# Attention weight gradients of a transformer backward pass: first loads moved into the last backward step, modulation gradients moved beside the last weight-gradient chunks

## Chip, cores, metric

One core of a Trainium2 chip. The metric is the device time of one execution in microseconds, lower is better; medians of several runs are given, and a profile of one execution of each kernel. The changed kernel and all experiments were measured against the kernel before on the same chip in alternating rounds. The rounds ran on several chips, so compare medians only within one round, and ratios across rounds.

## The reference

The program computes a forward pass and all its gradients: adaptive LayerNorm, an attention layer that walks over 64 segments of 32 tokens with 8 memory rows carried from segment to segment, and a gated feed-forward layer. Cut to what matters here:

```
q, k, v = h @ Wq, h @ Wk, h @ Wv         # 32 heads of 128, D = 512, rows h = 8 memory + 32 tokens
o = softmax(mask(q @ k.T)) @ v
out = o @ Wo ;  mem = out[:, :8]         # memory of the next segment
h = layernorm(x) * (1 + ca) + sa         # sa, ca, ... = silu(c) @ w_mod
# wanted here: dWo = o^T dy, dWq/dWk/dWv = h^T dq/dk/dv, dx through LayerNorm, dc, dw_mod
```

The backward pass over the segments is serial. When it has ended, the sums over all segments remain: the four weight gradients, the last LayerNorm's backward, and the gradients of `c` and `w_mod`. This last stage is what the change touches.

## The kernel before

PE = TensorE, DVE = VectorE, ACT = ScalarE, POOL = GpSimd, SP = SyncE. PSUM holds TensorE's sums in banks; an evacuation is the copy of a finished sum out of its bank by ACT or DVE. A load is issued by an engine's queue and has landed when all its data are there. "Half clock" is time in which TensorE was granted half of its clock. A backward step keeps the transposed weights in one pool:

```
self.WqT = wp.tile([128, H, D], BF16); self.WkT = ...; self.WvT = ...
self.WoT = wp.tile([128, DC, H * E], BF16)
```

The last stage (names: `dyrows` = gradient of the attention output by rows, `hrows` = attention input by rows, `rows` = per-head rows read from DRAM: OSR for o, DQR/DKR/DVR for dq/dk/dv):

```
hrows  = build_side_rows(self.H1ROWS, ...)      # 2.6 MB, half on SP's queue, half on ACT's
dyrows = build_side_rows(self.DAROWS, ...)      # 2.6 MB
load_rows(0); load_rows(1)                      # lp: three buffers of up to 2.6 MB
for i, (_, kind, outw, (hl, g0, ng)) in enumerate(todo):      # 9 o chunks, then 27 q/k/v chunks
    load_rows(i + 2)
    rows = loaded.pop(i)
    while ln_done[0] * len(todo) < i * NT and ln_done[0] < NT:
        ln_step()                               # one of 16 LayerNorm tiles
    if kind == "qkv":  ...                      # gps  <- hrows, rows  (4 x 20 matmuls of 128x512)
    else:                                       # gps5o <- dyrows, rows (20 matmuls a head)
        for gg in range(ng):
            ps = psG.tile([128, D], F32, tag="g")                        # 4 PSUM banks
            for tp_ in range(NTP):
                nc.tensor.matmul(ps[:], lhsT=rows[:, tp_, gg*E:(gg+1)*E], rhs=dyrows[:, tp_, :], ...)
            ot = op_.tile([128, D], BF16)                                # 3 output buffers
            self.evac(next_eng(), ot[:], ps[:])                          # ACT and DVE in turn
            nc.gpsimd.dma_start(outw[h0 + 3 * gg], ot[:])
...   # LayerNorm's last tiles, accs -> DMOD; pools close
...   # modulation gradients: dmod_bc, w_mod load; 4 x (dwm on DVE/ACT, junk on DVE); dc
```

One LayerNorm tile loads x0 (one DMA), dhb (eight small DMAs) and dx1 (one) on SP's queue, works on DVE, POOL and ACT, and adds two matmuls into a PSUM sum:

```
x0  <- x_rows;  bn_stats/bn_aggr/rstd/xh from x0
dhb <- DHA, DHB
nc.tensor.matmul(acc_ps, lhsT=sel[:, 0, :], rhs=dhb)
pr = dhb * xh                                   # POOL
nc.tensor.matmul(acc_ps, lhsT=sel[:, 1, :], rhs=pr)
dx1 <- DX1ROWS; dx0 = ln_bwd_rows(...); store
```

In these traces, what an engine is held by also holds what comes after it on the same engine (in e5 below, an evacuation stood 11.55 us behind load issues). The framework's scheduler decides that order from the source's order and from its own model of when data will be there.

## Time and profile before

| stage of the profiled run (us) | before |
|---|---|
| R, end of the last backward step (last dh_tps matmul) | 3051.2 |
| R to the first weight-gradient matmul | 47.8 |
| first to last weight-gradient matmul | 563.7 |
| of it, PE idle / at half clock | 1.0 / 4.7 |
| last matmul to the end of the span | 33.6 |
| R to the end of the span | 645.1 |

Median 3693.76 us of 3 runs (3689.59 to 3695.60). These dates are read from the instruction records of the trace. R itself moves by more than 10 us from one profile to the next, for reasons upstream (the seven steps before the last take 15 to 24 us each, not the same ones long each time). So all comparisons below use the time from R to the end, which no upstream scatter enters. Two profiles of the same changed kernel agree in it within 2 us; every other kernel has one profile, so a difference of 2 or 3 us between kernels says little.

### The profile page before, as it was taken

The numbers are of one execution on the slowest core, as the hardware profiler recorded it, in microseconds if no ns is written. First come the engines' busy times: TensorE is split into PE (matmuls) and PEld (weight loads), VectorE is DVE, ScalarE is ACT, GpSimd is POOL, SyncE is SP. The second block draws the span as 40 slices with busy tenths as digits, with TensorE's granted clock in tenths as the row PEclk, the third lists the DMA queues.
The fourth block names the chain that finished last, engine by engine and source line by source line (L and its number), as shares of the span: only waits on it lengthen the run. The fifth ranks groups of instructions, "written<-read, shape, count | busy, mean of one in ns | idle before, by whom it ended". The sixth has DMA issues, their size and how long they took to land.

```text
span 3696.3 us, 108208 instructions
## 1 busy us (share of the span) xinstructions
PE 3282.3 (89%) x45566; PEld 1897.6 (51%) x45566; DVE 1640.8 (44%) x4087; ACT 1208.9 (33%) x2742; POOL 957.9 (26%) x1917
## 2 busy tenths in 40 slices
PE   1889888899999969996989999999999994999996
PEld 1445444455555535553546666666666662445453
DVE  2454444455545556663225445444455541222222
ACT  0444444444544444442123333333333330000001
POOL 3333333333333323331111112111221221222221
PEclk6999999999999989998999999999999997999998
DMA  7565656566666653324779999999999998787774
GB/s 235 122 134 127 137 131 131 138 137 141 143 139 148 144 163 123 121 102 151 231 213 236 230 228 228 226 223 217 238 246 233 235 212 201 206 207 196 200 197 149
DMA packets 809259, 667.20 MB, mean 181 GB/s; under 512 B 511082, under 2 KB 683898, under 8 KB 808644
## 3 DMA queue, kind: packets, MB, share of 16 engines
q1 hardware_dynamic: 718948, 501.39, 60.5%
q0 software_dynamic: 31024, 103.06, 9.0%
q10 hardware_dynamic: 58800, 55.84, 5.8%
q8 instruction: 357, 5.85, 0.7%
q14 instruction: 130, 1.06, 0.1%
HBM read 292.82 MB, written 275.02 MB: 154 GB/s over the span
## 4 chain that ended last, share of the span: by engine, by line
PE 53%; DMA 5%; issue 3%; DVE 3%; ACT 1%; SPq 1%; POOL 0%; DVEq 0%; ACTq 0%; POOLq 0%
PE gps L1372 11%; PE dh_ps L208 10%; PE proj_ps L1138 6%; PE g_ps L1171 4%; PE gps5o L1382 3%; PE gps L941 3%; PE mm L855 3%; PE dh_tps L208 2%; PE tps L1103 2%; DMA Kst<-KST 2%; PE mm L788 1%; PE mm L792 1%; PE dp_ps L1161 1%; PE dp_ps L1157 1%; PE pass_ps L435 1%
## 5 line engine op out<-in xcount | busy, mean ns | idle before, releaser
L1372 PE MATMUL gps<-rows,hrows 128*128 128x512 bf16 (+2 forms) x2160 | 417.1, 355 | 0.0
L1372 PEld LDWEIGHTS <-hrows 128*128 128x128 bf16 x2160 | 211.4, 98 | 204.2
L647 POOL TENSOR_TENSOR Pst<-Pst,rden 120x1408 bf16<-120x1408 bf16 x64 | 162.7, 2542 | 415.4 <-DMA Pst<-ET 347.3
L1138 PE MATMUL proj_ps<-dyT,WoT 128*128 128x40 bf16 x8192 | 233.1, 180 | 19.4 <-issue 11.8
L1138 PEld LDWEIGHTS <-WoT 128*128 128x128 bf16 x8192 | 223.6, 96 | 30.6 <-issue 30.4
L63 DVE CAST ot<-gps 128x512 bf16<-128x512 f32 (+3 forms) x77 | 48.9, 635 | 395.2 <-PE gps L1372 259.7
L435 PEld LDWEIGHTS <-hT 128*32 128x32 bf16 x6144 | 140.5, 97 | 156.9 <-ACT hT L638 22.4
L234 DVE TENSOR_TENSOR dh_lo<-dh_ps,dh_hi 128x256 bf16<-128x256 f32 x128 | 48.4, 420 | 344.0 <-ACT dh_hi L230 344.0
L1382 PE MATMUL gps5o<-dyrows,rows 128*128 128x512 bf16 x640 | 141.4, 383 | 45.4 <-DMA rows<-OSR 45.4
L61 ACT ACTIVATE ot<-gps 128x512 bf16<-128x512 f32 (+3 forms) x77 | 42.4, 551 | 418.1 <-PE gps L1372 262.5
L208 PE MATMUL at_ps<-Wo,OT 128*32 128x512 bf16 x2048 | 135.0, 384 | 27.9 <-ACT OT L61 25.4
L61 ACT ACTIVATE dVT<-g_ps 128x512 bf16<-128x512 f32 (+1 forms) x192 | 107.8, 561 | 157.3 <-PE g_ps L1171 119.2
L208 PE MATMUL dh_ps<-WvT,dVT 128*32 128x512 bf16 x2048 | 151.8, 391 | 4.6 <-issue 4.5
L1376 POOL DMA_DIRECT2D out_dram<-ot x108 | 81.2, 752 | 281.9 <-DVE ot L63 153.5
L61 ACT ACTIVATE dOT<-proj_ps 128x480 bf16<-128x480 f32 (+2 forms) x192 | 68.4, 391 | 257.8 <-PE proj_ps L1138 250.5
L61 ACT ACTIVATE dQT<-g_ps 128x512 bf16<-128x512 f32 (+1 forms) x192 | 107.8, 561 | 125.1 <-PE g_ps L1171 125.1
L63 DVE CAST dKT<-g_ps 128x512 bf16<-128x512 f32 (+1 forms) x192 | 123.7, 644 | 44.0 <-PE g_ps L1171 43.2
L63 DVE CAST RAq<-pass_ps 128x512 bf16<-128x512 f32 x128 | 88.4, 691 | 121.8 <-PE pass_ps L435 121.8
L234 DVE TENSOR_TENSOR at_lo<-at_ps,at_hi 128x256 bf16<-128x256 f32 x128 | 48.4, 420 | 211.9 <-ACT at_hi L230 211.9
L61 ACT ACTIVATE OT<-tps 128x512 bf16<-128x512 bf16 (+1 forms) x192 | 101.0, 560 | 122.5 <-PE tps L559 91.1
L208 PE MATMUL dh_ps<-WkT,dKT 128*32 128x512 bf16 x2048 | 136.7, 388 | 0.0
L435 PE MATMUL pass_ps<-Wv,hT 128*32 128x512 bf16 x2048 | 126.8, 391 | 9.4 <-ACT hT L638 9.4
(364 smaller groups left out, 7230.7 us busy)
## 6 DMA issues: line engine op xcount, KB each, us to landing
OSR<-Ost SPq DMA_DIRECT2D x64, 352.0 KB
OT<-OT SPq DMA_DIRECT2D x64, 352.0 KB
PS<-Pst SPq DMA_DIRECT2D x64, 352.0 KB
OT_l<-OT SPq DMA_DIRECT2D x64, 352.0 KB
Pst_l<-PS SPq DMA_DIRECT2D x64, 352.0 KB
DVR<-rows_x POOLq DMA_DIRECT2D x64, 352.0 KB, 5.0
DKR<-rows_x POOLq DMA_DIRECT2D x64, 352.0 KB, 6.4
DQR<-rows_x POOLq DMA_DIRECT2D x64, 352.0 KB, 4.7
```

The lines of the kernel that those rows point to most:

```text
L61: return nc.scalar.activation(out, in_, AF.Copy)
L63: return nc.vector.tensor_copy(out, in_)
L208: self.nc.tensor.matmul(ps[32 * j:32 * j + 32, :], lhsT=lhsT, rhs=w, start=(n < 4), stop=(n >= total - 4), tile_position=(0, 32 * j))
L234: nc.vector.tensor_tensor(lo[:], ps[:, 256 * h:256 * h + 256], parts[h][:], op=ALU.subtract)
L435: nc.tensor.matmul(ps[32 * j:32 * j + 32, :], lhsT=lhs(c), rhs=rhs, start=(c == 0), stop=(c == DC - 1), tile_position=(0, 32 * j))
L647: nc.gpsimd.tensor_tensor(Pst[0:120, :, :], Pst[0:120, :, :], rden[:, :].unsqueeze(2).to_broadcast([120, G, 128]), op=ALU.mult)
L855: nc.tensor.matmul(hp[:], lhsT=xT[:, fc, :], rhs=wT[:, fc, :], start=(n == 0), stop=(n == 2 * FC - 1))
L941: nc.tensor.matmul(ps[:], lhsT=h2r[:, j, c * 128:(c + 1) * 128], rhs=xr[:, j, :], start=(j == 0), stop=(j == NT - 1))
L1138: nc.tensor.matmul(ps[:, g_, hl * L:(hl + 1) * L], lhsT=WoT[:, c, h * E:(h + 1) * E], rhs=dyT[:, c, :], start=(c == 0), stop=(c == DC - 1))
L1171: nc.tensor.matmul(ps[:, j, :], lhsT=lh[:, g * GW:(g + 1) * GW], rhs=rh[:, g * GW:(g + 1) * GW], start=True, stop=True)
L1372: nc.tensor.matmul(ps[:, 0:ng * E], lhsT=hrows[:, tp_, c * 128:(c + 1) * 128], rhs=rows[:, tp_, 0:ng * E], start=(tp_ == 0), stop=(tp_ == ...
L1382: nc.tensor.matmul(ps[:], lhsT=rows[:, tp_, gg * E:(gg + 1) * E], rhs=dyrows[:, tp_, :], start=(tp_ == 0), stop=(tp_ == NTP - 1))
```

## The change

Its intent: (1) put the transposed Wo first in the pool and the new row tiles over it, so that the first loads can start while the last backward step still runs; (2) load only what the first chunk needs (chunk 0 split into 2 + 2 heads) and bring hrows later, beside chunks 1 and 2; (3) run LayerNorm's 16 tiles over 31 chunks in place of 36 and do the modulation gradients, one step a chunk, beside the last six.

```diff
+        self.WoT = wp.tile([128, DC, H * E], BF16, name="WoT")
         self.WqT = wp.tile([128, H, D], BF16, name="WqT")
...
-        self.WoT = wp.tile([128, DC, H * E], BF16, name="WoT")
...
         with ExitStack() as ctx:
+            rp = ctx.enter_context(tc.tile_pool(name="p5g_r", bufs=1))
+            dyrows = rp.tile([128, NTP, D], BF16, name="dyrows")
+            rows_a = rp.tile([128, NTP, 2 * E], BF16, name="rows5a")
+            zrow = rp.tile([1, M // 2, D], BF16, name="zrow")
+            ...                                  # rows_a, then dyrows, on both queues, first of all
...
+            def mod_grads(step):                 # 0: accs -> DMOD, dmod_bc; 1..4: w_mod tiles; 5: dc
...
-                hrows = build_side_rows(self.H1ROWS, "hrows", mem_h)
-                dyrows = build_side_rows(self.DAROWS, "dyrows", mem_dy)
+                hrows = rp.tile([128, NTP, D], BF16, name="hrows")
+                o_chunks = [(0, 0, 2), (0, 2, 2)] + chunks[1:]
...
-                load_rows(0)
                 load_rows(1)
+                load_rows(2)
+                n_ln = len(todo) - 6
                 for i, ... in enumerate(todo):
                     load_rows(i + 2)
+                    if 1 <= i <= 2:
+                        load_h(i - 1)
                     rows = loaded.pop(i)
-                    while ln_done[0] * len(todo) < i * NT and ln_done[0] < NT:
+                    while ln_done[0] * n_ln < i * NT and ln_done[0] < NT:
                         ln_step()
+                    if i >= n_ln:
+                        mod_grads(i - n_ln)
...
-            ...                                  # the old modulation gradients behind the loop
```

## The prediction

> **What bounds the kernel now.** I read the page's 40 slices first. PE is at 8 or 9 tenths nearly everywhere; after the start the lowest digits are a 6 in slices 15 and 19 (not touched by this change), a 4 in slice 34 (3050 to 3142 us) and a 6 in the last. In these two something is waited for. I then read the chain that ended last in its last 650 us, which crosses both holes:
>
> ```profile
> 3045.83 5.37 PE dh_tps L208 x96
> 3051.64 12.98 DMA hrows<-H1ROWS
> 3064.64 2.77 DMA hrows<-AOA
> 3067.43 11.25 DMA dyrows<-DAROWS
> 3082.22 5.93 SPq L1357
> 3088.20 7.76 SPq L1357
> 3096.00 14.95 DMA x<-in_A_x_dram
> ...
> 3636.68 26.01 PE gps L1372 x160
> 3662.69 30.74 issue
> ```
>
> Columns: start, length (us), what. The last backward step ends at about 3051.2 (its tail matmuls, dh_tps). Then one load stands behind another (hrows, dyrows, rows) and PE does nothing until 3099.0. From there matmuls follow each other to 3662.7, and the last 31 us have none. Who waited, for the weight-gradient stage and then for the issue queue of SyncE at its start (total us, times, longest):
>
> ```profile
> PE gps5o L1382 <- DMA rows<-OSR: 45.4, 1, 45.4
> PE acc_ps L1288 <- POOL pr L1287: 1.0, 1, 1.0
> ...
> SPq L281 <- PE dh_tp L255: 8.0, 1, 8.0
> SPq L1336 <- DMA dyrows<-DAROWS: 8.0, 1, 8.0
> ```
>
> So the whole stage has one big wait, 45.4 us, and almost none later: 563.7 us from first to last matmul, about 2 of them lost. SyncE itself was held 8.0 us until 3051.24: its first load of this stage lies over the backward step's weights. The tail, from the timeline:
>
> ```profile
> 3662.81 0.35 SPq L1398 DMA_DIRECT2D dmod_bc<-DMOD  x1
> 3670.65 2.85 ACT L1407 ACTIVATE dwm<-dmod_bc,scT 128x3072 bf16<-128x3072 f32 x1 [7.56 <-DMA dmod_bc<-DMOD]
> 3677.79 3.36 DVE L1410 SCALAR_TENSOR_TENSOR junk<-wmod,dmod_bc 128x3072 bf16<-128x3072 bf16 x1 [5.32 <-DMA wmod<-in_w_mod_dram]
> 3689.36 3.35 DVE L1410 SCALAR_TENSOR_TENSOR junk<-wmod,dmod_bc 128x3072 bf16<-128x3072 bf16 x1
> 3693.97 0.28 SPq L1424 DMA_DIRECT2D out_dram<-dc_rows  x1
> ```
>
> The modulation gradients load only at 3662.8, though their input (accs stored to DMOD at 3637.4) was ready 25 us before: their pools open after the matmuls' pools close. Last matmul to end of span: 3696.3 - 3662.7 = 33.6 us.
>
> **What the Trainium skill says.** "DMA: Bandwidth & Descriptors", Queues, rings and completion order, says that SP and ACT each own a ring on the same 16 engines, served in turn; its Anatomy of one DMA says that a wait is done by the issuing sequencer before dispatch. So a load waiting in a queue holds all behind it, and two queues share bandwidth. The trace agrees: with one queue feeding, the windows show some 200 GB/s, with both 340:
>
> ```profile
> 3085.00:3087.00 2.00, 0.00 (x0) 0.00 (x0) 0.00 (x0) 0.00 (x0) 0.00 (x0) 0.50 1.15 203
> 3093.00:3095.00 2.00, 0.00 (x0) 0.00 (x0) 0.00 (x0) 0.00 (x0) 0.00 (x0) 0.50 1.10 346
> ```
>
> The same page's Specifications put line rate at transfers of 512 B or more. The trace differs a little: the 512 B pieces of a two-head chunk (3201 to 3205) moved at 255 GB/s, against 346 for 1 KB. The Anatomy's fixed 2 us also shows: an undisturbed 64 KB store took 2.1 us to land. "TensorE: Matmul & The Clock Gate", What's actually happening, gives about 3.4 us at half clock after idling; here the first 20 matmuls took 6.8 us (3099.0 to 3105.8) instead of 4.3. That is paid in both kernels.
>
> **The change, part by part.** (1) *Early loads over the freed dO weights.* The source puts WoT first in its pool and the new rows and dyrows tiles over it, so that they could load from 3032.5, where the last step finishes with WoT. The built program says otherwise: the first of these loads on SyncE waits for the last tail matmul against WqT, the very wait that held ca_bc until 3051.24, and ACT's half stands behind the last dh_b_hi evacuation (3051.5). I take the pools, not the tiles, to be what is waited for. So I give the early start nothing.
>
> (2) *What is loaded before the first matmul.* Before: hrows 2.62 MB, dyrows 2.62 MB and four heads of rows 2.62 MB, partly shared with the next chunk. After: two heads of rows (1.31 MB) and dyrows; hrows goes behind chunks 1 and 2. The clock: data flow from about 3053.3 (as H1ROWS did). Rows 1.31 MB at 255 GB/s: 5.1 us, to 3058.4. DAROWS 2.10 MB took 10.8 us from issue to landing both times before (H1ROWS: 3051.6 to 3062.4; DAROWS: 3067.4 to 3078); queued behind the rows without a gap it needs 7 us of flow, so it lands at about 3066. Then the small pieces: in the built program the loads of both queues take eight DMA semaphores in rotation, and each waits until its semaphore's last user has landed; so the second DHA piece on SyncE waits for ACT's DAROWS, ACT's zero row for SyncE's DAROWS. Before, that ending took 3 us of issues (3078 to 3081); now three DHA pieces and the zero row at 0.75 us each, to 3069, and 2.1 us to land: first matmul at 3071 instead of 3099.0. Gain 28.
>
> (3) *What is given back.* The first LayerNorm tile's matmul stands, in PE's order, after 154 of the stage's matmuls, i.e. 6.8 + 134 x 0.2165 = 35.8 us after the start, at 3106.8. Its dhb loads stand on SyncE behind hrows, and by the same rotation one waits for ACT's half of chunk 4, which ACT issues only after its second evacuation (about 3091.5) and behind its 1.05 MB half of H1ROWS. Estimate from the rates above: rows 1 to 3 (5.9 MB) to 3091, H1ROWS to 3097, ACT's half of chunk 4 (1.31 MB, one queue, 200 GB/s) to 3104 and landing 3105; two more waits of 2 to 2.5 us in the chain: dhb at 3110, pr 1 us later. PE waits about 5 us there, against 2 before. ACT, held by its hrows pieces until about 3108, still evacuates before PE needs the bank (four banks of 4.3 us). Later chunks have 17.3 us for 2.62 MB (151 GB/s), as before. Cost 3.
>
> (4) *Tail.* In the built program step 0 falls at chunk 30, the four w_mod steps around chunks 31 and 32 (two w_mod loads far earlier, among the dO-weight chunks), the final transpose before the last chunk. Per step ACT 2.85 us and DVE 3.4 us, while each evacuates one 0.6 to 0.7 us tile in 8.6: DVE was busy 2.9 of 26.7 us at the old end, so there is room. The added 1.57 MB broadcast and 6.3 MB of w_mod and out_11 fall in about 90 us in which DMA moved 160 GB/s: room too. What remains behind the last matmul is one evacuation (0.4), the issue (at +0.7) and the landing of a 64 KB store (2.1 to 2.5): 3.2 us instead of 33.6. Gain 30.4. (5) LayerNorm over 31 chunks instead of 40 and chunk 0 as 2+2 heads: the same matmuls, no cost.
>
> Sum: 28 - 3 + 30.4 = 55 us, 1.5%. 3693.8 - 55 = 3639.
>
> **Rivals.** (a) The loads do start at 3032.5: then rows and DAROWS land under the backward step, only DHA and the zero row remain after 3051.3, first matmul near 3059, time 3627. For it: source and title. Against: the built wait, which I trust; 5%. Even that stays within 2%. (b) The wait moves: LayerNorm's first tiles and the rows behind hrows starve PE by 10 to 15 us instead of 5, since 11 MB must pass in the first 45 us and two queues now wait for each other. For it: before, those tiles' loads stood behind nothing but rows; against: before, PE lost only 2 us with the DMA equally full. Time 3646 to 3651; 20%. (c) The modulation work stalls PE late: dmod_bc arrives late, ACT (which waits for it in order) holds its evacuations past four banks. For: DMOD's store queues behind 1.31 MB of rows. Against: I count 16 us from the accumulator's end to dmod_bc, with about 20 available before the evacuation behind it is due. 3 to 8 us; 15%. (d) Nothing gained in front because bandwidth is conserved: hrows' 2.62 MB must still move, but in about 140 us of dO-weight chunks which need 151 of 230 GB/s, so it hides. Against this rival; 5%.
>
> **Range and chances.** First matmul 3068 to 3076, given-back waits 0 to 12, end behind the last matmul 3 to 6, run scatter 3 each way: 3630 to 3650 should hold it 8 times in 10. 2% faster is 3619.9, a gain of 74; all idle time of both holes is 48 + 33.6 = 82, and the loads and the last store can't be free, so faster has 0.02. Slower would need a new 130 us: 0.01.
>
> **What would show it.** The first weight-gradient matmul at 3071, waiting for dyrows or its zero row, with SyncE's first load issued at 3051 and not at 3033 (else step 1 is wrong, rival a). One wait of PE of some 5 us for dhb about 36 us later (step 3). No PE wait above 2 us in the last 100 us, w_mod multiplies among the evacuations, and 3 to 4 us between last matmul and end (step 4). The prediction is wrong if PE's waits within the stage sum to over 15 us, or if a new wait stands at the first q chunk for hrows.

## The result, and the profile after

The changed kernel takes 3653.19 us (median of 4: 3650.16 to 3660.49) against 3694.68 (4 runs). The ratio is 0.9893, with a 95% interval of 0.9874 to 0.9911. Ratios here are the mean time of one kernel's runs over that of the other's of the same rounds, so not quite the ratio of the medians. In later rounds the same kernel took 3662.09 (6 runs) against 3691.24, ratio 0.9910 [0.9879, 0.9940]. It is 1% faster, where 1.5% was predicted, and the first median lies 3 us above the predicted range.

| us | before | after | after, repeated | predicted |
|---|---|---|---|---|
| R to first matmul | 47.8 | 23.5 | 19.9 | 19.8 |
| first to last matmul | 563.7 | 581.6 | 583.1 | 567 |
| PE idle in it | 1.0 | 13.9 | 15.5 | 5 |
| at half clock in it | 4.7 | 15.7 | 15.3 | as before |
| last matmul to end | 33.6 | 4.2 | 4.2 | 3.2 |
| R to end | 645.1 | 609.3 | 607.3 | 590 |

The gain from R to the end is 35.8 us (24.3 - 17.9 + 29.4) in the first profile and 37.8 in the second. The span of the first profile is 47 us shorter than before's; the 11 us beyond the 35.8 are R, which came earlier there. The two ratios, which take in all runs and the stages before R, come to 39 and 33 us, so there is no sign that the change gained or lost anything before R.

The chain that ended last, kernel after, its longest pieces before 3125, same columns as before:

```profile
3040.93 15.09 DMA dyrows<-DAROWS
3064.00 27.47 DMA rows<-OSR
3092.98 9.69 DMA x<-in_A_x_dram
3110.95 13.71 DMA rows<-OSR
```

The end of the backward step is followed by one 15 us load of dyrows, where before there were hrows, dyrows and rows in a row. But the chain does not then go over to matmuls, as it did before: it goes on, with short pieces between, through loads until after 3124. The waits, first of SyncE's queue around the stage's start, then of PE over the whole stage:

```profile
SPq L1263 <- PE dh_tp L255: 8.9, 1, 8.9
SPq L275 <- DMA hrows<-H1ROWS: 5.3, 1, 5.3
```

```profile
PE gps5o L1423 <- DMA dyrows<-zrow: 20.7, 1, 20.7
PE acc_ps L1304 <- POOL pr L1303: 5.8, 4, 2.6
PE acc_ps L1301 <- DMA hrows<-AOA: 4.7, 1, 4.7
PE acc_ps L1301 <- DMA dhb<-DHB: 1.8, 2, 1.2
```

The first load (line 1263) waited until the last step had ended, so nothing started early. Line 275 is the first piece of LayerNorm's dhb: SyncE could not issue it for 5.3 us, until an H1ROWS load had landed. The one big wait is 20.7 us instead of 45.4. New are the small ones, nearly all at LayerNorm's two matmuls (lines 1301 and 1304); by their dates all of 0.6 us or more lie in the first 130 us after R. The longest, in the timeline of DVE, ACT and PE:

```profile
3102.69 0.69 DVE L1290 BATCH_NORM_STATS2 st<-x 128x6 f32<-128x512 bf16 x1 [12.65 <-DMA x<-in_A_x_dram]
3105.24 0.60 ACT L61 ACTIVATE ot5o<-gps5o 128x512 bf16<-128x512 f32 x1 [19.96 <-DMA hrows<-AOA]
3105.64 0.58 PE L1301 MATMUL acc_ps<-dhb,sel 128*128 128x512 bf16 x1 [4.74 <-DMA hrows<-AOA]
3108.49 0.58 PE L1304 MATMUL acc_ps<-pr,sel 128*128 128x512 bf16 x1 [1.41 <-POOL pr L1303]
```

DVE stands 12.65 us for x0 and PE 4.74 us for dhb; ACT is idle for 20 us, the last 11.5 or so behind its own hrows issues (an estimate: the sum that it evacuates was complete at about 3093.7, 4.3 us after the one before). The releaser named for PE's wait is the transfer that arrived last by the profile; the matmul itself reads dhb. The eight pieces of dhb were issued from 3099.7 to 3103.8, behind the 5.3 us shown above and behind hrows, whose first issue alone held SyncE's queue for 9.32 us (0.53 us for the other half on ACT's queue). After it the matmuls run at half clock until 3113. The engines and the transfers in 10 us windows of the kernel after (busy times, then granted clock, DMA share, GB/s):

```profile
3070.00:3080.00 10.00, 9.13 (x43) 3.99 (x42) 0.69 (x1) 0.60 (x1) 1.08 (x2) 1.00 1.14 285
3080.00:3090.00 10.00, 9.87 (x46) 4.31 (x46) 1.35 (x2) 0.60 (x1) 1.08 (x2) 1.00 1.10 298
3090.00:3100.00 10.00, 9.95 (x47) 4.56 (x47) 0.03 (x1) 0.00 (x0) 0.54 (x1) 1.00 1.09 248
3100.00:3110.00 10.00, 3.63 (x11) 1.17 (x10) 5.64 (x13) 1.41 (x2) 2.86 (x4) 0.66 0.64 140
```

and of the kernel before, at about the same distance from its first matmul (3099.0):

```profile
3110.00:3120.00 10.00, 10.00 (x48) 4.57 (x47) 5.42 (x15) 1.68 (x3) 1.99 (x4) 1.00 0.27 87
3130.00:3140.00 10.00, 10.00 (x48) 4.51 (x46) 5.45 (x12) 1.29 (x2) 4.14 (x7) 1.00 0.49 129
```

After, the DMA share is 1.1 for 30 us on end while the o chunks run and PE then runs dry. Before, the windows at 0.27 and 0.49 stand between others at 1.05 to 1.10. Over the first 90 us after R the mean share is 0.82 before and 0.97 after, the rate 203 and 220 GB/s. (A share of 1.1 is no fixed rate: in the prediction's two windows it went with 203 and with 346 GB/s.) The tail, kernel after:

```profile
3645.22 0.38 ACT L61 ACTIVATE ot<-gps 128x256 bf16<-128x256 f32 x1 [3.98 <-PE gps L1413]
3645.89 0.72 POOL L1417 DMA_DIRECT2D out_dram<-ot  x1 [1.37 <-ACT ot L61]
```

One evacuation and one store end the program, as predicted.

### The profile page after: what moved, and what is told of

The parts are those of the page before. It is cut to its first block, busy times and chain, and to the rows that moved or that the text cites. A ratio compares the mean times of both kernels' runs of the same rounds, so it can differ in the third digit from the quotient of the medians.

```text
span 3649.4 us, 108148 instructions
## 1 busy us (share of the span) xinstructions
PE 3275.7 (90%) x45490; PEld 1897.2 (52%) x45566; DVE 1636.2 (45%) x4085; ACT 1214.5 (33%) x2744; POOL 963.1 (26%) x1917
## 4 chain that ended last, share of the span: by engine, by line
PE 42%; DMA 11%; issue 6%; DVE 4%; POOL 2%; ACT 2%; SPq 0%; ACTq 0%; POOLq 0%; DVEq 0%
PE dh_ps L208 10%; PE proj_ps L1138 6%; PE g_ps L1171 4%; PE gps L941 3%; PE mm L855 3%; PE dh_tps L208 2%; PE gps5o L1423 2%; PE tps L1103 2%; DMA rows<-DKR 2%; DMA Kst<-KST 2%; PE gps L1413 1%; PE mm L788 1%; DMA x<-in_A_x_dram 1%; PE mm L792 1%; PE dp_ps L1161 1%
## 5 line engine op out<-in xcount | busy, mean ns | idle before, releaser
L63 DVE CAST dKT<-g_ps 128x512 bf16<-128x512 f32 (+1 forms) x192 | 123.4, 643 | 37.8 <-PE g_ps L1171 37.4
L1423 PE MATMUL gps5o<-dyrows,rows 128*128 128x512 bf16 x588 | 133.0, 384 | 1.8 <-DMA rows<-OSR 0.8
L435 PE MATMUL pass_ps<-Wq,hT 128*32 128x512 bf16 x2048 | 134.0, 382 | 0.0
```

The lines of the kernel that those rows point to most:

```text
L63: return nc.vector.tensor_copy(out, in_)
L435: nc.tensor.matmul(ps[32 * j:32 * j + 32, :], lhsT=lhs(c), rhs=rhs, start=(c == 0), stop=(c == DC - 1), tile_position=(0, 32 * j))
L1423: nc.tensor.matmul(ps[:], lhsT=rows[:, tp_, gg * E:(gg + 1) * E], rhs=dyrows[:, tp_, :], start=(tp_ == 0), stop=(tp_ == NTP - 1))
```

## The experiments

18 kernels ran on the chip. Totals of one kernel scatter by some 10 us either way (the kernel before: 3678 to 3713 in all rounds). "Idle" is PE's idle time between first and last weight-gradient matmul, split into the first 90 us after R, the rest of the o chunks, and the q/k/v chunks (gaps of some 0.2 us are left out, so the split can sum to half a microsecond less than the totals in the text). The last column is the ratio to the kernel before with its 95% interval.

| kernel | R to first | idle: 90 us / rest of o / qkv | half clock | first to last | last to end | R to end | median us | ratio |
|---|---|---|---|---|---|---|---|---|
| before | 47.8 | 1.0 / 0 / 0 | 4.7 | 563.7 | 33.6 | 645.1 | 3694.68 | 1 |
| after | 23.5 | 9.3 / 3.8 / 0.3 | 15.7 | 581.6 | 4.2 | 609.3 | 3653.19 | 0.9893 [0.9874, 0.9911] |
| e19_after (the same) | 19.9 | 12.9 / 2.5 / 0 | 15.3 | 583.1 | 4.2 | 607.3 | 3662.09 | 0.9910 [0.9879, 0.9940] |
| e1_tail | 50.6 | 1.0 / 2.1 / 9.9 | 12.0 | 580.3 | 4.2 | 635.1 | 3679.58 | 0.9966 [0.9939, 0.9993] |
| e2_front | 22.9 | 7.2 / 2.7 / 0 | 10.9 | 575.5 | 32.4 | 630.9 | 3675.14 | 0.9954 [0.9930, 0.9978] |
| e3_lnlate | 19.9 | 7.5 / 0 / 12.1 | 15.4 | 588.4 | 4.2 | 612.4 | 3659.72 | 0.9916 [0.9889, 0.9943] |
| e4_hlate | 19.8 | 11.1 / 4.9 / 1.3 | 24.5 | 587.7 | 4.2 | 611.7 | 3657.76 | 0.9914 [0.9887, 0.9941] |
| e5_early | 15.9 | 10.9 / 0.9 / 8.9 | 21.6 | 591.5 | 4.2 | 611.6 | 3665.10 | 0.9932 [0.9906, 0.9958] |
| e6_pre | 19.9 | 14.0 / 2.0 / 7.8 | 22.3 | 594.0 | 4.3 | 618.1 | 3668.51 | 0.9934 [0.9908, 0.9960] |
| e9_defer | 20.0 | 13.3 / 0 / 6.5 | 21.6 | 589.5 | 4.2 | 613.7 | 3660.34 | 0.9912 [0.9888, 0.9936] |
| e7_bufs | 20.0 | 12.3 / 5.5 / 0 | 24.0 | 588.3 | 4.3 | 612.6 | 3656.29 | 0.9898 [0.9873, 0.9924] |
| e12_noload | 20.4 | 11.6 / 0 / 0.4 | 16.2 | 580.5 | 4.2 | 605.1 | 3648.15 | 0.9876 [0.9861, 0.9891] |
| e13_nowork | 23.0 | 7.5 / 9.0 / 6.5 | 25.9 | 592.9 | 4.4 | 620.2 | 3665.85 | 0.9927 [0.9905, 0.9949] |
| e14_poolq | 20.1 | 15.7 / 11.3 / 10.2 | 31.5 | 614.3 | 4.2 | 638.6 | 3682.80 | 0.9980 [0.9947, 1.0013] |
| e15_shift4 | 19.9 | 8.5 / 7.6 / 0.8 | 16.9 | 584.8 | 4.2 | 608.9 | 3659.69 | 0.9895 [0.9865, 0.9926] |
| e16_fewrows | 23.0 | 5.9 / 0 / 0 | 12.8 | 571.6 | 4.2 | 598.9 | 3639.20 | 0.9873 [0.9841, 0.9905] |
| e17_best | 19.5 | 13.3 / 0 / 0.3 | 21.5 | 582.7 | 4.2 | 606.4 | 3659.56 | 0.9915 [0.9892, 0.9937] |
| e18_spread | 19.9 | 10.4 / 3.6 / 11.4 | 35.2 | 600.0 | 4.3 | 624.2 | 3677.21 | 0.9956 [0.9927, 0.9984] |
| e20_spread6 | 20.1 | 11.9 / 3.6 / 1.4 | 21.2 | 587.9 | 4.3 | 612.3 | 3655.35 | 0.9896 [0.9848, 0.9944] |
| e21_tail6 | 50.4 | 1.0 / 0 / 2.7 | 5.4 | 567.3 | 4.3 | 622.0 | 3674.96 | 0.9944 [0.9899, 0.9989] |

All are correct except e12, e13 and e16.

### Taking the change apart: e1_tail, e2_front

e1 is the kernel before with only the modulation part and its denser LayerNorm; e2 the kernel after with only the front.

```diff
 # e1, on before
-    while ln_done[0] * len(todo) < i * NT ...
+    while ln_done[0] * n_ln < i * NT ...          # n_ln = 30 of 36 chunks
+    if i >= n_ln: mod_grads(i - n_ln)
 # e2, on after
-    n_ln = len(todo) - 6
+    n_ln = len(todo)
-    if i >= n_ln: mod_grads(i - n_ln)             # done behind the loop, as before
```

> The kernel before with the tail part of the change alone (modulation gradients beside the last six chunks, LayerNorm over 30 chunks instead of 36; loads at the front as before). Theory A (the changed kernel loses its missing 14 us to waits of TensorE for the first LayerNorm tiles, whose loads stand behind hrows): nothing is lost here, the 33.6 us behind the last matmul become about 4, gain 29 to 30 us, ratio 0.992, waits of TensorE inside the stage under 4 us. Theory B (packing LayerNorm more densely or the modulation work itself starves TensorE): gain 15 to 20 us, with 10 us or more of new waits for dhb, pr or PSUM banks.

> The changed front alone (two heads and dyrows first, hrows behind chunks 1 and 2), the tail as before with LayerNorm over all 37 chunks. Theory A: the first matmul comes about 24 us sooner, then the same waits of 12 to 14 us for dhb and pr plus some 3 us at half clock; net gain 6 to 10 us, ratio about 0.998. Theory B: no such waits, since LayerNorm is spread thinner; net gain 20 to 25 us, ratio 0.994.

The tail alone removes 29.4 us behind the last matmul, as in the whole change, but gives 16.6 back between the first and the last, mostly in the q/k/v chunks (waits for PSUM banks, taken up below). The front alone brings the first matmul 24.9 us forward and gives 11.8 back, all in the o chunks, although its LayerNorm runs over 37 chunks. So the front's waits don't need the denser LayerNorm. Neither theory gave the size: the tail alone gains 10.0 us from R to the end, the front alone 14.2.

### Moving one load or the other out of the front: e3_lnlate, e4_hlate

```diff
 # e3
-    while ln_done[0] * n_ln < i * NT ...
+    while ln_done[0] * (n_ln - 8) < (i - 8) * NT ...
 # e4
-    if 1 <= i <= 2: load_h(i - 1)
+    if 5 <= i <= 6: load_h(i - 5)
```

> The changed kernel with the LayerNorm tiles starting 8 chunks later (over 23 chunks instead of 31), hrows still behind chunks 1 and 2. Theory A: the waits for dhb and pr (12 us in the trace of the changed kernel) and the half clock after them (3 us) go, 12 to 16 us faster than the changed kernel, about 3638 us, first matmul unchanged at 23 us after the last backward matmul. Theory B: denser LayerNorm makes it worse, 0 to 10 us slower than the changed kernel. Theory C (bandwidth: too many bytes in the first 100 us): half of the gain, since LayerNorm is a tenth of those bytes: waits for rows appear instead.

> The changed kernel with hrows loaded behind chunks 5 and 6 instead of 1 and 2; LayerNorm as in the changed kernel. Theory A: the 4.7 us wait for dhb at the first LayerNorm tile and the half clock after it go; a part returns at the tiles beside chunks 5 to 7, where hrows now stands; 6 to 12 us faster than the changed kernel. Theory B: unchanged within 3 us.

My first theory, that LayerNorm's first loads are late because hrows stands in front of them, falls with e4: hrows is gone from there, and the first LayerNorm tile still waits 6.6 us for dhb, another 4.2. In e3 the LayerNorm waits are gone from the front, but a wait for rows stays there and others come in the q/k/v chunks; PE's waits over the stage:

```profile
PE gps L1413 <- DVE ot L63: 6.6, 3, 3.2
PE gps L1413 <- ACT ot L61: 5.6, 2, 4.1
PE gps5o L1423 <- DMA rows<-OSR: 4.5, 1, 4.5
```

### The early start made real: e5_early

```diff
+        wo = ctx.enter_context(tc.tile_pool(name="p4wo", bufs=1))
+        self.WoT = wo.tile([128, DC, H * E], BF16, name="WoT")
         wp = ctx.enter_context(tc.tile_pool(name="p4w", bufs=1))
-        self.WoT = wp.tile([128, DC, H * E], BF16, name="WoT")
...
-            zrow = rp.tile(...); hrows = rp.tile(...)
+            zp = ctx.enter_context(tc.tile_pool(name="p5g_z", bufs=1))
+            zrow = zp.tile(...); hrows = zp.tile(...)
```

> The changed kernel with its pools cut apart: the dO weights in a pool of their own, dyrows and rows5a in a pool that fits inside them, the zero row and hrows in another. In the built program the first loads now wait only for the last proj_ps matmul over the dO weights, not for the last matmul over WqT. If the prediction's step (1) is right (the early start is lost because one pool spans both weights), the first rows5a load issues some 8 to 12 us before the backward step's end, and the first gps5o matmul comes 8 to 13 us after that end instead of 23.5; stage from the backward step's end to the span's end 597 to 603 us against 609.3. If transfers are the limit of the front (rival), the first matmul stays at 18 us or later. The waits at the first LayerNorm tiles should stay as they are in both (11 to 17 us of PE idle).

The pool was the obstacle: cut apart, the loads start during the last step, and the first matmul follows R by 15.9 us instead of about 20 (a smaller gain than the 8 to 13 us after R that were expected), and R to the end is 611.6 us, not 597 to 603. The last step itself, before R, now takes 32.4 us in place of 21.8. ACT's timeline and PE's waits there:

```profile
3054.07 10.51 ACTq L1271 DMA_DIRECT2D dyrows<-DHA  x4
3064.63 0.66 ACT L230 ACTIVATE dh_hi<-dh_ps 128x256 bf16<-128x256 f32 x2 [11.55 <-DMA dyrows<-DHA]
```

```profile
PE dh_ft L243 <- ACT dh_hi L230: 8.7, 1, 8.7
```

ACT issues four DHA loads. The second could not be issued for 6.0 us and the third for 0.8, until DAROWS loads had landed, and the evacuation dh_hi that the step needs stands behind them in ACT's order. The 4 to 8 us won at the first matmul are lost before R. In this form, with DHA on ACT's queue, the early start makes the kernel no faster; no run tried it with those loads elsewhere.

### Is it the order of LayerNorm's work? e6_pre, e9_defer, e7_bufs

```diff
 # e6: x0, dhb, dx1 of tile j+1 loaded in step j; LayerNorm one chunk later
+    ln_load(ln_done[0]); ln_load(ln_done[0] + 1)
     ln_tile(ln_done[0])
 # e9: the two matmuls of tile j issued in step j+1
-    nc.tensor.matmul(acc_ps, lhsT=sel[:, 0, :], rhs=dhb ...)   # and pr
+    pend.append((j, dhb, pr))
 # e7
-    op_ = tile_pool(name="p5g_o", bufs=3)
+    op_ = tile_pool(name="p5g_o", bufs=6)
```

> The changed kernel with the three loads of each LayerNorm tile (x0, dhb, dx1) issued one LayerNorm step ahead, the first before the second rows load; LayerNorm starts one chunk later. Theory L (LayerNorm's loads come late, and what stands behind them in the order of VectorE, ScalarE and TensorE is held): PE idle inside the chunks falls from 13.9 to under 5 us, half-clock time from 15.7 to under 9, chunks 581.6 -> 565 to 571, stage from the backward step's end 595 to 601 against 609.3. Theory B (LayerNorm's and the modulation's own work on VectorE and GpSimd, packed into fewer chunks): PE idle stays at 10 us or more, stage 605 or more.

> The changed kernel with only the two TensorE matmuls of each LayerNorm tile (into acc_ps) moved one LayerNorm step later; loads and all other work unchanged. If the waits are only TensorE's own order (it stands at a LayerNorm matmul whose dhb or pr is late, while the evacuations have room), PE idle falls from 13.9 to under 4 us and the stage to 595 to 600. If VectorE's and ScalarE's evacuations are held as well (by x0's load, by the loads that ScalarE issues itself), the waits come back as waits for PSUM banks: PE idle 7 to 14 us, stage 602 to 610.

> The changed kernel with six output buffers (ot, ot5o) in place of three. Rival O (evacuations wait for a buffer whose store has not landed: the profile after has 113 us of such ScalarE idle and 94 us of VectorE idle): PE idle falls by half or more, to under 7 us, stage under 603. Theory L: those waits have slack, PE idle stays at 11 to 17 us and the stage at 606 to 612.

None lowers the idle time. In e6 the LayerNorm loads are ahead, the first tile comes without a wait 45.7 us after R, and PE waits for rows instead (11.0 us in two waits, the longer 6.8). The scheduler also moved the first work of the next tile forward with its load, so that VectorE still stood 90 us in 14 waits for x0: a load issued earlier was simply awaited earlier. In e9 PE waits 4.2 us for rows and 5.6 at the first LayerNorm matmul. e7 shows that the three output buffers are not what holds the front. Whatever went first in these runs, something else was late by as much.

### Loads or work? e12_noload, e13_nowork, e14_poolq

```diff
 # e12 (wrong on purpose): all tiles use tile 0's x0, dhb, dx1; all work and stores stay
-    x0 = sb2.tile(...); nc.sync.dma_start(x0, ...)   # dhb, dx1 likewise
+    x0, dhb, dx1 = fixed
 # e13 (wrong on purpose): all loads and the store stay; the work is one addition on GpSimd
-    bn_stats ... xh, pr, ln_bwd_rows
+    nc.gpsimd.tensor_tensor(dx0b, x0, dx1, op=ALU.add)     # second matmul reads dhb
 # e14: LayerNorm's loads, but tile 0's, on GpSimd's queue
-    nc.sync.dma_start(x0 ...)
+    nc.gpsimd.dma_start(x0 ...)
```

> Wrong results on purpose: the changed kernel, but every LayerNorm tile works on the three loads (x0, dhb, dx1) of the first tile; all work on VectorE, ScalarE, GpSimd and TensorE, and the stores, stay. If the waits come from LayerNorm's loads, late or in the way of the row loads, PE idle inside the chunks falls from 13.9 to under 6 us (the first tile still waits), the chunks from 581.6 to 566 to 573 us and the stage from the backward step's end from 609.3 to 594 to 601. If LayerNorm's own work in the engines' order holds the evacuations, PE idle stays at 10 us or more and the stage at 605 or more.

> Wrong results on purpose, the reverse: every LayerNorm tile makes its three loads and its store, one addition on GpSimd in place of all other work, and its two matmuls both read dhb. If the loads are the cause, PE idle stays at 9 to 15 us and the stage at 603 to 611. If the work is, PE idle falls under 6 us and the stage to 594 to 601.

> The changed kernel with LayerNorm's loads on GpSimd's queue instead of SyncE's, but for the first tile. If those loads are late because they stand in SyncE's order behind row loads that wait for a buffer or an earlier transfer, PE idle falls to 5 to 8 us (the first tile's wait of 4.7 stays), the stage to 598 to 603. If the transfer engines are simply full in the first 60 us, the waits stay in sum, 12 us or more, and the stage 606 or more; it may lose on top of that, by GpSimd's issues standing in front of the output stores.

e13 clears LayerNorm's work as the main cause: without it PE idles 23 us. Its second tile alone waits 9.0 for dhb. That is above the 9 to 15 expected, 6.5 of it being one wait for ACT in the q/k/v chunks. e12 is the half answer. After the first tile LayerNorm costs almost nothing more, but these waits stay:

```profile
PE acc_ps L1308 <- DMA hrows<-AOA: 5.8, 1, 5.8
PE gps5o L1428 <- DMA rows<-OSR: 3.4, 1, 3.4
```

so idle is 12.0, not under 6, and the stage 605.1, not below 601: LayerNorm's later loads are worth 2 to 4 us of the stage, hardly more than two profiles of one kernel differ. e14 is much worse (37 us idle). The Trainium skill, "DMA: Bandwidth & Descriptors", Issuing engines are not separate DMA queues, says that transfers from all issuing engines end up on the same 16 DMA engines. The run agrees in so far as another queue did not relieve the front: its first 90 us have 15.7 us of idle, and GpSimd's loads now stand in front of its `pr` and its stores.

### Fewer bytes in the front, and tries at a better version: e16_fewrows, e15_shift4, e17_best, e18_spread, e19_after

```diff
 # e16 (wrong on purpose): chunks 2 to 5 read chunk 1's rows again, no loads for them
+    if 2 <= i <= 5: loaded[i] = kept[0]; return
 # e15: LayerNorm 4 chunks later, six output buffers
+    while ln_done[0] * (n_ln - 4) < (i - 4) * NT ...
 # e17: LayerNorm 2 chunks later and over 33, hrows at chunks 5 and 6, six output buffers, and e18's tail
 # e18: modulation over the last four chunks, LayerNorm over 33
-    n_ln = len(todo) - 6
+    n_ln = len(todo) - 4                          # steps (0), (1,2), (3,4), (5)
```

> Wrong results on purpose: the changed kernel, but chunks 2 to 5 use the rows loaded for chunk 1 again, so that 9 to 10 MB of row loads fall out of the first 100 us. If the front is short of transfers, the eighth o head is evacuated 56 to 65 us after the backward step's end in place of 71.4, and PE idle in the o chunks falls from 13.6 to 6 us or less. If the order of the loads or LayerNorm's own work holds the front, the date stays at 69 to 75 us.

> A try at a better version: LayerNorm's first tile four chunks later (its 16 tiles over chunks 5 to 31) and six output buffers. If the front is short of transfers, PE idle in the first nine chunks falls from 13.9 to 5 us or less and, unless the denser tiles make VectorE hold the evacuations later as in the run with eight chunks' delay (437.6 us after the o chunks), the stage comes to 597 to 603. If the denser tiles cost as much again, 608 to 613.

> A try at a better version: LayerNorm two chunks later and over 33 chunks, hrows loaded at chunks 5 and 6, the modulation work over the last four chunks, six output buffers. If the order of the loads is what holds the front, the eighth head comes at 60 to 66 us and the stage at 595 to 601 us. If the front is short of transfers, the eighth head stays at 69 to 75 us and the stage at 603 to 610.

> The changed kernel with LayerNorm's 16 tiles over 33 chunks in place of 31 and the modulation work over the last four. If the density of LayerNorm costs by itself, PE idle falls by 3 to 6 us and the stage to 603 to 606; if only the front does, both stay (12 to 16 us, 607 to 612). If four chunks are too few for the modulation work, the time after the last gradient matmul grows from 4.2 to over 8 us.

> The changed kernel again, unaltered, to see how its stage numbers repeat: PE idle 10 to 18 us, first gps5o matmul 19 to 24 us after the backward step's end, stage 606 to 613 us, and a ratio of 0.986 to 0.992.

e16 is the only kernel with the change's front whose idle time falls below half. PE's waits after the start:

```profile
PE acc_ps L1301 <- DMA dhb<-DHB: 4.9, 1, 4.9
PE acc_ps L1304 <- POOL pr L1303: 1.0, 1, 1.0
```

The waits for rows and those of the second to fourth LayerNorm tile are gone; only the first tile's remains. First to last matmul is 571.6 us, 10 to 11.5 less than in the two profiles of the kernel after. One expectation missed: the eighth head's evacuation still came at 71.7 us, because here the first matmul came 3 us later than in the repeat and the scheduler had put two LayerNorm tiles before that head. The gain shows behind it. The bytes moved in the first 90 us after R fell only from 19.8 to 18.3 MB (220 and 203 GB/s), at the same mean share of 0.97, since later loads moved up into the room. So what e16 removes is the row loads that PE needs there, and that others stand behind, and not the load on the transfers. e15 and e17 reorder the same bytes, and idle stays at 16.9 and 13.6 us; e17 did bring the eighth head to 64.9 us, as the theory of order said, but lost 8.4 us at its second LayerNorm tile 20 us later. Neither is faster than the kernel after: in the rounds that they shared, e17 took 3659.56 us and e19 3662.09. e18, with *less* dense LayerNorm, is 15 us slower in the stage, so density as such is not what costs.

### The waits for PSUM banks in some kernels: e20_spread6, e21_tail6

Eight kernels lost 6 to 12 us in the q/k/v chunks; the kernel after, twice, did not. Both runs change only the output buffers of a kernel that did:

```diff
-    op_ = tile_pool(name="p5g_o", bufs=3)
+    op_ = tile_pool(name="p5g_o", bufs=6)
```

> The run with LayerNorm over 33 chunks, with six output buffers in place of three and nothing else. If the buffers caused the waits for banks, the time from the first hrows matmul to the last gradient matmul falls from 436.3 to 423 us or less and the stage from 624.2 to 606 to 612. If not (the evacuations are held by LayerNorm's own loads in VectorE's order), it stays at 428 or more.

> The kernel before with the tail part alone, with six output buffers in place of three and nothing else. If the buffers caused the waits for banks, the time from the first hrows matmul to the last gradient matmul falls from 434.1 to 423 us or less and the stage from 635.1 to 618 to 625 (the kernel before's 645.1 less the tail's 29, plus the front waits of 3 us). If not, it stays at 428 or more.

PE's waits in the q/k/v chunks, e1 and then e21:

```profile
PE gps L1412 <- DVE ot L63: 9.1, 3, 5.0
```

```profile
PE gps L1412 <- DVE ot L63: 1.9, 1, 1.9
```

VectorE's waits there, e18 and then e20:

```profile
DVE ot L63 <- DMA out_dram<-ot: 104.9, 15, 9.7
...
DVE st L1290 <- DMA x<-in_A_x_dram: 65.5, 8, 17.0
```

```profile
DVE st L1290 <- DMA x<-in_A_x_dram: 77.6, 8, 15.6
```

From the first hrows matmul to the last gradient matmul, 436.3 us became 421.9 and 434.1 became 423.2 (0.2 over the limit set); R to the end fell to 612.3 (expected 606 to 612) and 622.0. With six buffers VectorE still stands for x0, no shorter than before, but no longer for a buffer whose store hasn't landed, and PE's waits for banks all but go. So the buffers are needed for this loss. That the stop for x0 is its other half is read from these waits; no run removed it. Each kernel has one profile here, and the ratios alone don't separate e21 from e1, nor quite e20 from e18.

## Why the prediction was right or wrong, step by step

**Step 1, no early start: right.** SP's first load waited for the last matmul of the backward step. e5 shows that the pool was the reason, and that rival (a), as e5 built it, did not bring its 3627.

**Step 2, the first matmul at R + 19.8, a gain of 28: right in most profiles, though not in the first.** Of the 16 profiles with the change's front and its pools uncut, 12 have it at 19.5 to 20.4 us and 4 at 22.9 to 23.5; the kernel after itself did both. The difference didn't matter, because of what the step left out, the next load: the rows for the second half of chunk 0 landed 35 to 36 us after R in either case. PE waited 4.7 us for them where it had started at 19.9, and 0.8 where it had started at 23.5. Start plus this wait is 24.6 and 24.3, so at that point the front is worth some 23 us.

**Step 3, "Cost 3": the step that failed, by its size.** Predicted was one wait of some 5 us for the first LayerNorm tile's dhb, less 2 that the kernel before loses too. That wait came at the expected place in PE's order, 4.7 + 1.4 us, partly by luck: measured from R, PE was predicted to reach it at 55.6 us and dhb to land at 58.8, and they came at 60.8 and 65.6 (62.0 and 66.9 in the repeat), both late. The kernel before lost 1.0 there and not 2. But the wait was not alone. In the repeat of the kernel after: 4.7 for rows, 4.9 + 1.0 at the first LayerNorm tile, 4.8 at the second to fourth, 15.5 in all, 14.5 more than before; and 10.6 us more at half clock, at half speed worth 5.3 (an estimate; a little of it is idle time counted twice). The sum, 19.8, accounts for the 19.4 us by which the chunks grew. In the first profile it is 12.9 + 5.5 = 18.4 against 17.9. The prediction had set the half-clock time equal in both kernels; but a wait of 4.7 us in mid-stage pays it again: the granted clock is half until 3113.4.

The cause is settled in part. It is late loads and not LayerNorm's work (e13), and none of the orders tried got the time back (e4, e6, e9 and e17 rearrange them, and 13.6 to 24.0 us of idle time stay). Taking 9.8 MB of row loads out of the front returns 10 to 11.5 us (e16), taking LayerNorm's loads after the first tile returns 1 to 3 (e12). The front of the change starts PE some 25 us earlier against much the same bytes, with a DMA share of 1.1 for 30 us. The prediction knew this as rivals (b), given 20%, whose 10 to 15 us of waits are what came (13.9 and 15.5), and (d), given 5%, and dismissed (d) with 151 GB/s needed of 230 over 140 us of o chunks. That is an average over the stage; most of the waits sit in its first 90 us, in which three chunks are loaded ahead together with hrows. Not separated is the rate of the transfers from the way they are issued. The trace shows an issue, and all behind it on its queue, held until an earlier load with no tile in common has landed, as the prediction's eight semaphores in rotation have it: the first tile's dhb stood 5.3 us on SyncE for H1ROWS in the kernel after, 4.0 us for AOA in e16. No run gave those loads semaphores of their own; e6 put the first tile's in front, where they came in time and PE waited for rows, and e14 moved only the later tiles' to another queue. So the 5 to 7 us of the first LayerNorm tile stay open: they come in every kernel with this front, e16 too, but for e6, which loads that tile first, e17, and e3 and e15, which put it later; in these as much is lost elsewhere.

**Step 4, the tail: right.** 4.2 us for 3.2, gain 29.4 for 30.4, and no stall of PE in the last chunks (rival c did not come).

**Step 5, the denser LayerNorm "no cost": right for this kernel, by luck.** The same or nearly the same density went with a loss of 9 to 14 us in the q/k/v chunks of e1, e5 and e9; for e1 six output buffers removed most of it (e21), for e5 and e9 that was not tried. (The step also speaks of 40 chunks before; there were 36.)

**The sum.** Predicted 28 - 3 + 30.4 = 55; measured 24.3 - 17.9 + 29.4 = 35.8. Of the missing 19.6, 14.9 are step 3, 3.7 step 2, and 1.0 the tail. So the term that failed is what is given back: 17.9 us, 19.4 in the repeat, for the 3 predicted.

## What to carry to other kernels

When loads are moved from in front of a stage to beside its first part, ask what the transfers must deliver in that part alone, not over the stage: here some 70% of the time won at the first matmul was lost again within 130 us of R, and none of the orders tried got it back. A load moved to the queue of an engine that also evacuates can hold that engine's later work, so an early start can delay the very step it hides behind (e5). A wait that only costs slack today (output buffers behind stores) is worth a second look before work is packed more densely beside it: three more buffers were worth 11 to 14 us in two of the variants and nothing in the kernel that had the slack.

## What the Trainium skill lacked or had wrong

- "DMA: Bandwidth & Descriptors", Anatomy of one DMA, has a wait done by the issuing sequencer before dispatch, but doesn't say what that does to an engine that also computes: in the kernel after some 11.5 of 20.0 us in which ScalarE was idle before an evacuation lay behind its own DMA issues, and in e5 an evacuation that stood behind four load issues (11.55 us idle) held PE 8.7 us.
- No page has the length of an issue on a queue that has transfers under way: H1ROWS' half on SyncE's queue took 9.32 us in the kernel after, right behind three row loads, and 3.29 us in e16, behind one; the other half on ScalarE's queue took 0.53 and 0.79 us.
- No page has a rate for two queues that carry pieces of 256 B to 1 KB at once. In the front of the kernel after, three 10 us windows with a DMA share of 1.09 to 1.14 moved 285, 298 and 248 GB/s. An estimate of such a front is better started from these than from the 346 of 1 KB pieces alone.
